# Unit 0's q and k in two parts of their tokens, and later prefetch loads, in a planned attention-and-MLP kernel

## Chip, cores and metric

The kernel runs on one core of one Trainium2 chip. The metric is the device time of one execution in microseconds (us); lower is better. Five runs of the kernel before stand beside one profiled execution of it.

## What is computed

Attention with a squared ReLU in place of the softmax, over 8 batches, 12 heads, 448 tokens and 64 columns a head; then an MLP with a squared ReLU over the 3584 tokens of all batches. Inputs and output are float32.

```python
scores = q @ k.T / sqrt(64)                      # per batch and head, 448 x 448
attn   = maximum(scores, 0) ** 2 / 448
x      = attn @ v                                # heads side by side: 3584 x 768
g      = maximum(x @ w_in, 0) ** 2               # w_in  768 x 2048
out    = g @ w_out                               # w_out 2048 x 768
```

## The kernel before

**Units and rounds.** Four heads of one batch are a unit; there are 24 units, three to a batch. Of a unit, 64 groups of seven consecutive tokens lie on partitions, so a unit has seven rounds, one for each token t of the group. q and k are loaded as float32 (raw, 448 KB each), cast to float16 (blk), and turned so that the 64 head columns lie on partitions (qkt). A round of scores (L453) multiplies one t of k by the turned q, the ReLU (L480 on VectorE or L483 on ScalarE) writes rel, the square (L487 on ScalarE or L489 on GpSimd) writes at, and the product with v (L518) collects in PSUM until it is copied to xt (L538, L540). The first MLP product of a batch reads xt (L580; L629 for the first columns of batch 0) and its squared ReLU goes to g; the second (L729 for batch 0, L794 later) makes the output, which SP's queue stores (L675).

**Three ways to load q and k.** Unit 0 is loaded by `load_qk` (L345): k on SP's queue, q on ScalarE's. Each is cast by one instruction on VectorE or ScalarE (`cast_qk`, L372), and turned on TensorE by `turn_pe` (L392, seven transposes into PSUM, in one or two calls, then a copy to qkt, L395). Units 1 to 5 are loaded by `load_early` (L362) on GpSimd's queue, which casts on the way. Units 6 to 23 are loaded by `load_qk` on SP's queue, cast on GpSimd and turned by a DMA transpose on SP's queue (`turn_dma`, L408). There are 4 raw buffers, 3 blk and 6 qkt. v and the weights come by GpSimd's queue, too (L422, L427, L432).

**The opening.** For the first 21 rounds (units 0 to 2) the query columns are worked in two parts (`PARTS`): the first 128, of the tokens QA = 0 and 1, four rounds together (the `quads`, with `tile(0, ...)`), and the other 320, of QB, a round at a time (`tile(1, ...)`). The first quad so needs tokens 0 to 3 of k and 0 and 1 of q of unit 0. The second quad needs unit 1's k and q as well.

**Zero and filler products.** Ahead of everything TensorE multiplies twelve tiles of zeros (L929, 512 columns). Until 45 us on the planner's clock, whenever it has nothing to do, a filler product of zeros (L932, 256 columns) is put in.

**The order of work.** `Plan` decides it when the program is built. Every operation has costs on the engines that can do it, dependencies, buffers, a due time, and perhaps a time `after` which it may start. TensorE's due times are `plan.now`, a running sum of costs that the `at` arguments move forward; others follow backwards from what needs them. `simulate` walks through time, gives each free engine the ready operation that is due first, and so writes the order of every queue; `land` works out when each DMA lands, from queues that share 400 KB a us and an allowance at the end, and the two are repeated five times. The times in the plan are costs of the planner, not measurements. The initial `busy` times, `{"PE": 6.25, ...}`, say from when an engine is free.

**Prefetch.** In the main loop over pairs of rounds i, `coming(n)` estimates when unit n's scores are due:

```python
def coming(n):
    return plan.now + 4.5 * (TJ * n - 2 * i) / 2
...
raws[n, w] = load_qk(n, w, max(50.0, coming(n) - 26.0), n < 8)
```

The last argument gates the loads of units 6 and 7 behind a small memset on GpSimd (L342), since their raw buffers may hold early data. On the planner's clock `coming` is 65.7 for unit 6, 75.4 for unit 7, 83.9 for unit 8 and 95.8 for unit 9, so the loads of units 6 and 7 may start at 50, those of unit 8 at 57.9 and those of unit 9 at 69.8. A load also needs a free raw buffer, which the cast of an earlier unit leaves.

Of the kernel before, what the change touches and what calls it, by code (L numbers as in the profile page):

```python
# [42 lines left out]
class Plan:  # L43
# [54 lines left out]
    def land(self):  # L98


        queues: dict = {}
        for op in sorted((op for op in self.ops if op.size), key=lambda op: op.start):
            queues.setdefault(op.engine, deque()).append([op.start + 1.3, op.size, op])
        now, idle = 0.0, set(queues)
        while queues:
            for name in idle & set(queues):
                if queues[name][0][0] <= now + 1e-9 and set(queues) - idle:
                    queues[name][0][0] = now + 2.3
                    idle.discard(name)
            live = [name for name in queues if queues[name][0][0] <= now + 1e-9]  # L110
            idle -= set(live)
            if not live:
                now = min(q[0][0] for q in queues.values())
                continue
            rate = 400e3 / len(live)
            step = min(queues[name][0][1] / rate for name in live)
            later = [q[0][0] - now for q in queues.values() if q[0][0] > now + 1e-9]
            step = min([step] + later)
            now += step
            for name in live:  # L120
                q = queues[name]
                q[0][1] -= rate * step
                if q[0][1] <= 1e-3:
                    self.landing[q.popleft()[2].id] = now + (1.2 if len(queues) > 1 else 0.9)
                    if not q or q[0][0] > now + 1e-9:
                        idle.add(name)
            queues = {name: q for name, q in queues.items() if q}
# [133 lines left out]
def kernel(  # L261
# [9 lines left out]
    nc = tc.nc  # L271

    B, H, S, D = q.shape
# [42 lines left out]
        "s": fixed(psum, "sp", 2, [P, 2, 512], FP32),  # L316
        "mm": fixed(psum, "mm", 4, [P, 512], FP32),
    }
    plan = Plan(pools, {"PE": 6.25, "ACT": 0.7, "DVE": 1.2, "POOL": 1.4, "SP": 0.7})
    plan.cold = 6.6  # L320

    def act(n, emit):
# [7 lines left out]
    def load_qk(n, w, after=0.0, gate=False):  # L330
        b, u = divmod(n, NU)
        buf = Buf("raw")

        def tile_of():
            return buf.tile

        src = (q if w == "q" else k)[b, 4 * u:4 * u + 4].rearrange(
            "(f e) (p t) d -> (e p) f (t d)", e=2, t=TJ)
        deps = []
        if gate:  # L340
            deps.append(plan.add(
                [("POOL", 0.1, 0.1, lambda: nc.gpsimd.memset(buf.tile[0:1, 0, 0:1], 0.0))],  # L342
                bufs=[buf], after=after))
        eng, name = (nc.scalar, "ACT") if (n, w) == (0, "q") else (nc.sync, "SP")
        op = plan.add([(name, 0.5, 0.5, lambda: eng.dma_start(out=tile_of(), in_=src), QK)],  # L345
                      deps, [buf], after=after)
        return op, buf, tile_of

    def load_early(n, w, after, due):

        b, u = divmod(n, NU)
        z = 2 * n - 2 + (w == "q")
        buf = early if z < NH else Buf("raw")

        def view():
            if z < NH:
                return early.tile[:, 2 * z:2 * z + 2]
            return buf.tile[:, 0].bitcast(FP16).rearrange("p (f c) -> p f c", f=2)

        src = (q if w == "q" else k)[b, 4 * u:4 * u + 4].rearrange(  # L360
            "(f e) (p t) d -> (e p) f (t d)", e=2, t=TJ)
        op = plan.add([("POOL", 0.7, 0.7, lambda: nc.gpsimd.dma_start(out=view(), in_=src), QK)],  # L362
                      [], [buf], after=after, due=due)
        return op, buf, lambda t: [
            (slice(64 * f, 64 * f + 64), view()[:, f, t * D:(t + 1) * D]) for f in range(2)]

    def cast_qk(n, w, raw, names=("POOL",)):
        load, buf, tile_of = raw
        blk = Buf("blk")

        def emit(fn):
            return lambda: fn(blk.tile.rearrange("p t (f d) -> p f t d", f=2),  # L372
                              tile_of().rearrange("p f (t d) -> p f t d", d=D))

        alts = {"POOL": ("POOL", 0.88, 0.93, emit(nc.gpsimd.tensor_copy)),
                "DVE": ("DVE", 0.56, 0.63, emit(nc.vector.tensor_copy)),
                "ACT": ("ACT", 0.85, 0.94, emit(nc.scalar.copy))}
        return plan.add([alts[x] for x in names], [load], [buf, blk]), blk, (
            lambda t: [(slice(0, P), blk.tile[:, t, :])])
# [545 lines left out]
    idle = pools["part"][0].bitcast(FP16)[:, 0:512]  # L925
    nc.vector.memset(idle, 0.0)
    make_identity(nc, ident)
    for _ in range(12):
        nc.tensor.matmul(pools["mm"][3], lhsT=idle[:, 0:P], rhs=idle, start=True, stop=True)  # L929

    plan.fill_until = 45.0
    plan.filler = lambda bank: nc.tensor.matmul(  # L932
        bank[:, 0:256], lhsT=idle[:, 0:P], rhs=idle[:, 0:256], start=True, stop=True)

    early = Buf("g")
    raws, casts = {}, {}
    for w in "kq":
        raws[0, w] = load_qk(0, w)
    plan.add([("ACT", 1.3, 1.3, lambda: None)], [raws[0, "q"][0]], due=2.0)
    for w in "kq":  # L940
        casts[0, w] = cast_qk(0, w, raws[0, w], ("DVE", "ACT"))
    for w in "kq":
        casts[1, w] = load_early(1, w, 1.4, 1.0)
    load_v(0, 1.4, 1.1)
# [4 lines left out]
    w1_ops = [load_w1(0, 1.4, 1.5)]  # L949
    w1_ops += [load_w1(i, 8.0, 1.6) for i in range(1, 4)]  # L950

    QA, QB = range(0, 2), range(2, TJ)
    rounds = [divmod(r, TJ) for r in range(STREAM)]
    first_h = deque(h_first())
    held: dict = {}
# [11 lines left out]
    def tile(part, rs, at=None):  # L967
        cols = PARTS[part]
        w = cols.stop - cols.start
        sp = Buf("s")  # L970
        op = scores(rs, [sp], cols, True, at)
        second, at = square(op, sp, len(rs) * w, "at" if part else "comb")
        for j, (n, t) in enumerate(rs):
            def view(tl, j=j, w=w, part=part):
                if not part:
                    tl = tl.rearrange("p f c -> p (f c)").rearrange("p (e c) -> p e c", e=2)
                return tl[:, :, j * w:(j + 1) * w]
            held[part, n, t] = second, at, view

    quads = [rounds[r:r + 4] for r in range(0, STREAM, 4)]  # L980
    turn_pe(0, "k", casts[0, "k"], 5.6)
    turn_pe(0, "q", casts[0, "q"], None, QA)
    for i, rs in enumerate(quads):
        tile(0, rs, 7.0 + 1.2 * i)
        if i in (0, 1):
            turn_pe(i + 1, "k", casts[i + 1, "k"])
            turn_pe(i + 1, "q", casts[i + 1, "q"], None, QA)
        if i:
            put(0, quads[i - 1])
    for n in range(NU):  # L990
        turn_pe(n, "q", casts[n, "q"], None, QB)
    tile(1, rounds[0:1])
    put(0, quads[-1])
    tile(1, rounds[1:2])
# [26 lines left out]
    def coming(n):  # L1021
        return plan.now + 4.5 * (TJ * n - 2 * i) / 2

    skipped, chain = 0, None
    for i in range(STREAM // 2, NB):
        rs = [divmod(r, TJ) for r in range(max(STREAM, 2 * i), 2 * i + 2)]
        for n in range(NU, NUN):
            if i == max(STREAM // 2, TJ * (n - 2) // 2 + 1):
                if n > 5:
                    for w in "kq":  # L1030
                        raws[n, w] = load_qk(n, w, max(50.0, coming(n) - 26.0), n < 8)
                if n > 5:
                    load_v(n, coming(n) - 6.0)
            if i == max(STREAM // 2, (TJ * (n - 1) + 1) // 2 - 2) and n > 3:
                if n >= NPE:
                    for w in "kq":
                        casts[n, w] = cast_qk(n, w, raws[n, w])
                if n < NPE:
                    for w in "kq":
                        turn_pe(n, w, casts[n, w])  # L1040
                else:
                    for w in "kq":
                        turn_dma(n, w, casts[n, w])
        todo = []
        for n, t in rs:
            sp = Buf("s")
            op = scores([(n, t)], [sp], WHOLE, False)
            todo.append((op, sp, n, t))
            if chain is not None:
                chain.glue = op  # L1050
            chain = op
        for op, sp, n, t in todo:
            second, at = square(op, sp, S)
            ats[n, t] = second, at, lambda tl: tl
        if i in avs:
            chain.glue = av(avs[i], list(range(TJ)))
            chain = chain.glue
        if i in pushes:
            push_dense(pushes[i])
        if i in avs and MERGE and i + 1 < NB:  # L1060
            skipped = 1
            continue
        nxt = min([j for j in pushes if j > i] or [NB + 2])
        run_some(max(0.0, (queued - 4.0) * (1 + skipped) / (nxt - i + skipped)))
        skipped, chain = 0, None
# [38 lines left out]
```

## Time and profile before

| what | value |
|---|---|
| median of 5 runs | 388.93 us (388.13 to 393.08) |
| the profiled execution | 388.46 us, span 386.7 us, mean granted TensorE clock 0.997 |
| TensorE busy | 376.5 us (97%) |
| ScalarE / VectorE / GpSimd busy | 277.0 / 266.3 / 173.8 us (72 / 69 / 45%) |
| chain that ended last | TensorE 89%, DMA 4%, VectorE 3%, ScalarE 2% |
| DMA | 51.34 MB, mean 133 GB/s |
| unit 0's k and q | issued at 0.75, landed after 4.3 and 4.6 us |
| first scores / first ReLU | 7.64 / 8.11 us |
| filler products (L932) | 46, from 5.98 to 36.9 us |

Times in the trace count from the start of the span. A share of busy time is an average over stages with different limits, so a stage is read by the work and the waits in it. A filler product counts as busy. SPq is SP's queue, in which a DMA's time is the time to issue it; when it lands is told apart.

### The profile page before, as it was taken

How to read it: one execution, taken by the hardware profiler on the slowest of the kernel's cores; microseconds unless marked ns; L12 is line 12 of the kernel's file. 1: busy time of each engine (PE TensorE's matmuls, PEld its weight loads, DVE VectorE, ACT ScalarE, POOL GpSimd, SP SyncE). 2: the span in 40 equal slices, each digit the busy share in tenths (PEclk: the TensorE clock that was granted, in tenths of full speed). 3: DMA queues.
4: the chain of work that ended last, by engine and by line, in shares of the span. 5: the costliest groups of instructions: out<-in, count | busy, mean ns of one | idle time of the engine just before them, and what ended most of it. 6: DMA issues, size and time to landing. Idle time of an engine off the chain costs nothing.

```text
span 386.7 us, 8379 instructions
## 1 busy us (share of the span) xinstructions
PE 376.5 (97%) x3324; PEld 200.1 (52%) x3324; DVE 266.3 (69%) x387; ACT 277.0 (72%) x413; POOL 173.8 (45%) x171
## 2 busy tenths in 40 slices
PE   8899999799999999999999999999999999999995
PEld 4556565345555445544555555544455546555563
DVE  3778789587886777676986674676886676256731
ACT  4999899598768787688876687795886785244221
POOL 8757447577745763654644643442601431001000
PEclk9999999999999999999999999999999999999998
DMA  9999998993566777667378576477472002210243
GB/s 194 198 207 190 204 262 217 193 225 94 143 128 173 158 168 132 163 163 166 51 208 165 107 172 168 90 153 179 65 115 61 3 2 53 65 26 3 56 96 94
DMA packets 69671, 51.34 MB, mean 133 GB/s; under 512 B 36864, under 2 KB 69632, under 8 KB 69632
## 3 DMA queue, kind: packets, MB, share of 16 engines
q1 hardware_dynamic: 52112, 35.86, 38.2%
q0 software_dynamic: 16928, 14.09, 25.0%
q10 hardware_dynamic: 592, 0.85, 0.7%
q8 instruction: 26, 0.43, 0.5%
q14 instruction: 13, 0.11, 0.1%
HBM read 45.61 MB, written 11.01 MB: 146 GB/s over the span
## 4 chain that ended last, share of the span: by engine, by line
PE 89%; DMA 4%; DVE 3%; ACT 2%; issue 1%; POOL 0%; POOLq 0%; DVEq 0%
PE mm L580 37%; PE mm L794 29%; PE sp L453 10%; PE mm L518 8%; DMA qkt<-blk 2%; PE mm L932 2%; DMA g<-in_q_dram 2%; DVE comb L773 1%; PE mm L629 1%; PE mm L729 1%; DVE rel L480 1%; PE mm L392 1%; ACT at L487 1%; ACT rel L483 0%; DVE part L806 0%
## 5 line engine op out<-in xcount | busy, mean ns | idle before, releaser
L580 PE MATMUL mm<-xt,w 128*128 128x448 f16 (+1 forms) x768 | 149.0, 346 | 0.0
L489 POOL TENSOR_TENSOR at<-rel 128x896 f16<-128x896 f32 (+1 forms) x49 | 79.9, 1630 | 106.2 <-ACT rel L483 84.7
L564 DVE SCALAR_TENSOR_TENSOR g<-mm,g 128x448 f16<-128x448 f32 (+1 forms) x128 | 76.7, 604 | 52.6 <-ACT g L569 52.2
L487 ACT ACTIVATE at<-rel 128x896 f16<-128x896 f32 (+1 forms) x119 | 108.2, 930 | 3.5 <-PE mm L518 2.4
L580 PEld LDWEIGHTS <-w 128*128 128x128 f16 x768 | 72.1, 98 | 70.6 <-issue 12.3
L480 DVE TENSOR_SCALAR rel<-sp 128x896 f32<-128x896 f32 (+2 forms) x86 | 89.0, 1039 | 19.8 <-PE sp L453 17.9
L569 ACT ACTIVATE g<-mm 128x448 f16<-128x448 f32 (+1 forms) x128 | 67.9, 534 | 42.8 <-PE mm L580 42.3
L483 ACT ACTIVATE rel<-sp 128x896 f32<-128x896 f32 (+2 forms) x88 | 79.2, 908 | 9.1 <-PE sp L453 8.2
L794 PEld LDWEIGHTS <-comb 128*128 128x128 f16 x416 | 39.8, 98 | 29.9 <-issue 3.7
L453 PE MATMUL sp<-qkt,qkt 64*64 64x448 f16 (+2 forms) x756 | 51.0, 338 | 3.1 <-DMA qkt<-blk 2.8
L713 ACT ACTIVATE part<-mm 128x384 f32<-128x384 f32 x40 | 19.6, 489 | 41.0 <-PE mm L794 39.3
L372 POOL CAST blk<-raw 128x896 f16<-128x896 f32 x36 | 37.7, 1058 | 23.6 <-issue 13.7
L806 DVE SCALAR_TENSOR_TENSOR part<-mm,part 128x384 f32<-128x384 f32 x52 | 28.6, 554 | 24.7 <-ACT part L713 14.7
L794 PE MATMUL mm<-wt,comb 128*128 128x384 f16 x208 | 36.8, 326 | 0.2 <-DVE comb L773 0.2
L794 PE MATMUL mm<-w,comb 128*128 128x384 f16 x208 | 36.8, 326 | 0.1
L518 PE MATMUL mm<-at,vs 64*64 64x448 f16 (+1 forms) x672 | 35.3, 343 | 0.0
L794 PEld LDWEIGHTS <-g 128*128 128x128 f16 x264 | 25.1, 98 | 19.2 <-issue 3.1
L453 PEld LDWEIGHTS <-qkt 64*64 64x64 f16 x756 | 17.7, 105 | 29.0 <-issue 24.8
L422 POOL DMA_DIRECT2D vs<-in_v_dram x48 | 29.7, 627 | 4.7 <-PE sp L453 3.7
L794 PE MATMUL mm<-w,g 128*128 128x384 f16 x176 | 30.9, 326 | 0.0
L695 POOL COPY rest<-g 128x1024 f16<-128x1024 f16 x8 | 9.8, 1228 | 44.1 <-DVE g L564 44.1
L518 PEld LDWEIGHTS <-vs 64*64 64x64 f16 x756 | 22.0, 107 | 12.9 <-issue 3.3
(61 smaller groups left out, 219.2 us busy)
## 6 DMA issues: line engine op xcount, KB each, us to landing
out_dram<-part SPq DMA_DIRECT2D x108, 96.0 KB, 2.2
raw<-in_k_dram SPq DMA_DIRECT2D x19, 448.0 KB, 3.9
raw<-in_q_dram SPq DMA_DIRECT2D x18, 448.0 KB, 4.5
vs<-in_v_dram POOLq DMA_DIRECT2D x48, 112.0 KB, 4.1
w<-in_moe_w_in_dram POOLq DMA_DIRECT2D x4, 768.0 KB, 14.5
w<-in_moe_w_out_dram POOLq DMA_DIRECT2D x4, 768.0 KB, 12.3
g<-in_k_dram POOLq DMA_DIRECT2D x4, 224.0 KB, 11.3
g<-in_q_dram POOLq DMA_DIRECT2D x4, 224.0 KB, 9.8
```

Of the source, the lines that this page charges most:

```text
L372: return lambda: fn(blk.tile.rearrange("p t (f d) -> p f t d", f=2), tile_of().rearrange("p f (t d) -> p f t d", d=D))
L422: nc.gpsimd.dma_start(out=buf.tile[64 * r:64 * r + 64], in_=src[:, u, hs])
L453: nc.tensor.matmul(sp[64 * c:64 * c + 64, e, c0:c0 + w].rearrange("p (t c) -> p t c", c=TP), lhsT=kT[r, t, 64 * e:64 * e + 64], rhs=qT[r, ...
L480: dve(n, lambda: nc.vector.tensor_scalar(out=rel(), in0=sp.tile[:, :, 0:width], scalar1=0.0, scalar2=SK, op0=ALU.max, op1=ALU.mult)),
L483: act(n, lambda: nc.scalar.activation(out=rel(), in_=sp.tile[:, :, 0:width], func=AF.Relu, scale=SK))],
L487: act(n, lambda: nc.scalar.activation(out=dst(), in_=rel(), func=AF.Square)),
L489: lambda: nc.gpsimd.tensor_mul(dst(), rel(), rel()))],
L518: nc.tensor.matmul(banks[f].tile[64 * e:64 * e + 64, c0:c0 + w], lhsT=vs[r, e ^ c, t * D:(t + 1) * D], rhs=a[r, e, :], start=(t == 0), sto ...
L564: nc.vector.scalar_tensor_tensor(out=dst, in0=src, scalar=0.0, in1=dst, op0=ALU.is_gt, op1=ALU.mult)
L569: nc.scalar.activation(out=dst, in_=src, func=AF.Square)
L580: nc.tensor.matmul(bank.tile[:, c0:c0 + w], lhsT=w1[f // 4][:, m, f % 4 * P:(f % 4 + 1) * P], rhs=xts[b].tile[:, m, cols], start=(m == 0), ...
L794: nc.tensor.matmul(buf.tile[:, 0:HALF], lhsT=lhs()[:, j, :], rhs=w[:, j, :], start=(first and j == 0), stop=(j == NH - 1), skip_group_chec ...
```

## The change

Unit 0's q and k are loaded, cast and turned in two parts each: k in tokens 0 to 3 and 4 to 6, q in tokens 0 and 1 and 2 to 6 (`load_first`). Only q's first part is issued on ScalarE's queue; k's first, k's second and q's second part follow each other on SP's. Each part is cast by itself into one blk buffer and may be cast on VectorE or ScalarE. Turning is split in the same way: k's second part is turned behind the first quad. The zero products ahead fall from 12 to 9, and the planner holds TensorE free from 5.0 instead of 6.25. The due time of the first turn falls from 5.6 to 4.9 and those of the quads from 7.0 + 1.2 i to 5.8 + 1.2 i. The planner's placeholder for ScalarE's table load (1.3 us) no longer depends on q's load. The planner's allowance for a landing becomes 1.4 where it was 1.2 (several queues) or, after 12 us, 0.9 (one queue). The loads of units 6 to 23 may start at `coming(n) - 20` instead of `coming(n) - 26`. The other edits (`n > 5` for `n >= NPE`, QA and QB moved up) change nothing, since NPE is 6.

```diff
@@ -121,7 +121,8 @@
                 q = queues[name]
                 q[0][1] -= rate * step
                 if q[0][1] <= 1e-3:
-                    self.landing[q.popleft()[2].id] = now + (1.2 if len(queues) > 1 else 0.9)
+                    self.landing[q.popleft()[2].id] = now + (
+                        1.4 if len(queues) > 1 or now > 12.0 else 0.9)
                     if not q or q[0][0] > now + 1e-9:
                         idle.add(name)
             queues = {name: q for name, q in queues.items() if q}
@@ -316,7 +317,7 @@
         "s": fixed(psum, "sp", 2, [P, 2, 512], FP32),
         "mm": fixed(psum, "mm", 4, [P, 512], FP32),
     }
-    plan = Plan(pools, {"PE": 6.25, "ACT": 0.7, "DVE": 1.2, "POOL": 1.4, "SP": 0.7})
+    plan = Plan(pools, {"PE": 5.0, "ACT": 0.7, "DVE": 1.2, "POOL": 1.4, "SP": 0.7})
     plan.cold = 6.6
 
     def act(n, emit):
@@ -363,6 +364,30 @@
                       [], [buf], after=after, due=due)
         return op, buf, lambda t: [
             (slice(64 * f, 64 * f + 64), view()[:, f, t * D:(t + 1) * D]) for f in range(2)]
+
+    def load_first(w, parts):
+
+        raw, blk = Buf("raw"), Buf("blk")
+        src = (q if w == "q" else k)[0, 0:4].rearrange(
+            "(f e) (p t) d -> (e p) f (t d)", e=2, t=TJ)
+        for z, ts in enumerate(parts):
+            cols, ts = slice(ts[0] * D, (ts[-1] + 1) * D), slice(ts[0], ts[-1] + 1)
+            size = P * 2 * (cols.stop - cols.start) * 4
+            eng, name = (nc.scalar, "ACT") if (w, z) == ("q", 0) else (nc.sync, "SP")
+            load = plan.add([(name, 0.5, 0.5, lambda eng=eng, cols=cols: eng.dma_start(
+                out=raw.tile[:, :, cols], in_=src[:, :, cols]), size)], [], [raw],
+                due=-9.0 + 2 * z + (w == "q"))
+
+            def emit(fn, cols=cols, ts=ts):
+                return lambda: fn(
+                    blk.tile[:, ts].rearrange("p t (f d) -> p f t d", f=2),
+                    raw.tile[:, :, cols].rearrange("p f (t d) -> p f t d", d=D))
+
+            n = 2 * (cols.stop - cols.start)
+            casts[0, w, z] = plan.add(
+                [("DVE", 0.07 + 0.0008 * n, 0.15 + 0.0008 * n, emit(nc.vector.tensor_copy)),
+                 ("ACT", 0.09 + 0.00085 * n, 0.19 + 0.00085 * n, emit(nc.scalar.copy))],
+                [load], [raw, blk]), blk, lambda t: [(slice(0, P), blk.tile[:, t, :])]
 
     def cast_qk(n, w, raw, names=("POOL",)):
         load, buf, tile_of = raw
@@ -925,20 +950,20 @@
     idle = pools["part"][0].bitcast(FP16)[:, 0:512]
     nc.vector.memset(idle, 0.0)
     make_identity(nc, ident)
-    for _ in range(12):
+    for _ in range(9):
         nc.tensor.matmul(pools["mm"][3], lhsT=idle[:, 0:P], rhs=idle, start=True, stop=True)
 
     plan.fill_until = 45.0
     plan.filler = lambda bank: nc.tensor.matmul(
         bank[:, 0:256], lhsT=idle[:, 0:P], rhs=idle[:, 0:256], start=True, stop=True)
 
+    QS = QA, QB = range(0, 2), range(2, TJ)
+    KA = range(0, 4), range(4, TJ)
     early = Buf("g")
     raws, casts = {}, {}
-    for w in "kq":
-        raws[0, w] = load_qk(0, w)
-    plan.add([("ACT", 1.3, 1.3, lambda: None)], [raws[0, "q"][0]], due=2.0)
-    for w in "kq":
-        casts[0, w] = cast_qk(0, w, raws[0, w], ("DVE", "ACT"))
+    for w, parts in (("k", KA), ("q", QS)):
+        load_first(w, parts)
+    plan.add([("ACT", 1.3, 1.3, lambda: None)], [], due=2.0)
     for w in "kq":
         casts[1, w] = load_early(1, w, 1.4, 1.0)
     load_v(0, 1.4, 1.1)
@@ -949,7 +974,6 @@
     w1_ops = [load_w1(0, 1.4, 1.5)]
     w1_ops += [load_w1(i, 8.0, 1.6) for i in range(1, 4)]
 
-    QA, QB = range(0, 2), range(2, TJ)
     rounds = [divmod(r, TJ) for r in range(STREAM)]
     first_h = deque(h_first())
     held: dict = {}
@@ -978,17 +1002,19 @@
             held[part, n, t] = second, at, view
 
     quads = [rounds[r:r + 4] for r in range(0, STREAM, 4)]
-    turn_pe(0, "k", casts[0, "k"], 5.6)
-    turn_pe(0, "q", casts[0, "q"], None, QA)
+    turn_pe(0, "k", casts[0, "k", 0], 4.9, KA[0])
+    turn_pe(0, "q", casts[0, "q", 0], None, QA)
     for i, rs in enumerate(quads):
-        tile(0, rs, 7.0 + 1.2 * i)
+        tile(0, rs, 5.8 + 1.2 * i)
+        if not i:
+            turn_pe(0, "k", casts[0, "k", 1], None, KA[1])
         if i in (0, 1):
             turn_pe(i + 1, "k", casts[i + 1, "k"])
             turn_pe(i + 1, "q", casts[i + 1, "q"], None, QA)
         if i:
             put(0, quads[i - 1])
     for n in range(NU):
-        turn_pe(n, "q", casts[n, "q"], None, QB)
+        turn_pe(n, "q", casts[n, "q"] if n else casts[0, "q", 1], None, QB)
     tile(1, rounds[0:1])
     put(0, quads[-1])
     tile(1, rounds[1:2])
@@ -1028,11 +1054,11 @@
             if i == max(STREAM // 2, TJ * (n - 2) // 2 + 1):
                 if n > 5:
                     for w in "kq":
-                        raws[n, w] = load_qk(n, w, max(50.0, coming(n) - 26.0), n < 8)
+                        raws[n, w] = load_qk(n, w, max(50.0, coming(n) - 20.0), n < 8)
                 if n > 5:
                     load_v(n, coming(n) - 6.0)
             if i == max(STREAM // 2, (TJ * (n - 1) + 1) // 2 - 2) and n > 3:
-                if n >= NPE:
+                if n > 5:
                     for w in "kq":
                         casts[n, w] = cast_qk(n, w, raws[n, w])
                 if n < NPE:
```

## The prediction

> **What bounds the kernel now.** I read the busy table first, then the waits of TensorE, then the stretches, then the time-ordered list around the start and around the one long wait. TensorE is the bound by share:
>
> ```profile
> PE 376.5 (97%) x3324; PEld 200.1 (52%) x3324; DVE 266.3 (69%) x387; ACT 277.0 (72%) x413; POOL 173.8 (45%) x171
> ```
>
> Its 10.2 us of idle time are few pieces. The waits of TensorE (engine, line, releaser: us in total, times, longest):
>
> ```profile
> PE sp L453 <- DMA qkt<-blk: 2.8, 1, 2.8
> PE mm L929 <- DVE part L926: 1.2, 1, 1.2
> PE mm L518 <- issue: 1.1, 1, 1.1
> ```
>
> and some 4.7 us behind the last product, which the change does not touch. Busy is not useful, though: 12 products of zeros (L929) fill 1.20 to 6.15, and 46 filler products (L932), 0.11 apart, hold 5.0 us between 5.98 and 36.9. So up to 37 us TensorE waits in disguise; after that it has real work all the time but for the 2.8 us. The stretches (span, then busy us of PE, PEld, DVE, ACT, POOL, clock, DMA share, GB/s) say who sets the pace:
>
> ```profile
> 8.11:38.37 30.26, 28.65 (x503) 16.67 (x505) 22.95 (x34) 28.64 (x43) 21.35 (x26) 1.00 1.24 198
> 38.37:60.38 22.01, 22.01 (x262) 13.25 (x259) 18.48 (x30) 20.60 (x36) 11.71 (x14) 1.00 1.21 237
> 60.38:71.74 11.36, 8.59 (x62) 4.71 (x58) 8.94 (x10) 7.62 (x11) 4.99 (x6) 1.00 1.16 177
> 71.74:381.60 309.86, 309.64 (x2449) 162.03 (x2450) 212.96 (x310) 217.27 (x323) 128.99 (x113) 1.00 0.53 116
> ```
>
> From the first square to 38.37, where the last columns of batch 0 are copied into xt and the wide L580 products can begin, ScalarE is busy 28.64 of 30.26 us. It is the bound of the opening, and it starts late. From 38 us on only TensorE's work counts, and a hole.
>
> **The start, step by step.** In order of time (start, duration):
>
> ```profile
> 5.06 0.94 ACT L372 CAST blk<-raw 128x896 f16<-128x896 f32 x1 [2.50 <-DMA raw<-in_k_dram]
> 5.34 0.82 DVE L372 CAST blk<-raw 128x896 f16<-128x896 f32 x1 [4.20 <-DMA raw<-in_q_dram]
> 6.22 0.95 PE L392 MATMUL mm<-ident,blk 128*128 128x128 f16 x14
> 6.54 1.02 DVE L395 COPY qkt<-mm 128x256 f16<-128x256 f16 x2 [0.38 <-PE mm L392]
> 7.64 0.42 PE L453 MATMUL sp<-qkt,qkt 64*64 64x128 f16 x16
> 8.11 1.76 ACT L483 ACTIVATE rel<-sp 128x1024 f32<-128x1024 f32 x2 [0.21 <-PE sp L453]
> ```
>
> The first quad needs only four tokens of k and two of q. In the change those are 256 and 128 KB of the 896 KB. *Landing:* the 896 KB took 4.6 us from issue; a 96 KB store lands in 2.2 (median), so some 2.0 are fixed and 2.6 are data; 384 KB of the data are 1.1. The parts would then land at 0.75 + 3.1 = 3.85, against 5.34; if all four parts travel interleaved nothing is gained. I take 4.3, a gain of 0.75 to 1.0 with k as the later. *Cast:* 512 of 896 elements at 0.9 ns plus 0.1 is about 0.55 against 0.82 to 0.94: 0.3. *Turn:* 6 transposes instead of the 14 ahead of the scores: 0.35 against 0.83. But zeros run at half pace: the 512 columns of an L929 product come 0.43 apart, L932's 256 columns 0.11 apart. With 9 zeros real work starts at 1.20 + 9 x 0.43 = 5.05, probably before the pace doubles (it did between 5.4 and 6.0), so the six turns cost up to 0.64; I take 0.55: 0.3 gained. *Copy:* 512 and 256 wide instead of 896 and 256: 0.2. The sum is 1.55 to 1.8; first scores at about 6.1 instead of 7.64, and cutting three zeros (1.24 us) makes room for just that. The added work, two more loads, two more casts and one more copy, is some 0.1 to 0.15 of fixed time each on ScalarE and VectorE, which both idled before 8 us; the second k and q parts stand behind k's first in SP's queue, which has nothing else to issue before 51.79.
>
> What passes through? Quad 1 needs unit 1's q, issued on GpSimd's queue at 2.33 and landed at 8.23; that does not move. Until then ScalarE and VectorE can only take unit 0's own rounds, second part, which need q's late tokens. ScalarE at 95% means that an earlier first square is worth nearly its whole shift at 38 us, if the gap until 9.8 is filled. Bounds: 0 (quad 1 decides) and -1.5. I take -1.2.
>
> In sentences that nothing else rests on: the Trainium skill, "TensorE: Matmul & The Clock Gate" (Part 1: The HAM clock gate), says the array runs at half clock until it has been busy for a window of about 3.4 us. That speaks against fewer zeros; here half pace lasted until some 4.5 us of zeros, and by the rule, with the window unluckily placed, the first scores too would run at half pace, an estimated 0.3 us more, a start gain of 0.9. The same skill's "DMA: Bandwidth & Descriptors" (Bandwidth) wants transfers of 1 MiB or more and gives each a fixed 2.0 us; if these added up for SP's three parts, q's second part would land at an estimated 8.5 us and the start gain would be about half.
>
> **The hole.** Around it, SP's queue:
>
> ```profile
> 60.30 0.37 SPq L345 DMA_DIRECT2D raw<-in_k_dram  x1
> 60.77 1.33 SPq L408 DMA_TRANSPOSE qkt<-blk  x1
> 62.19 0.52 SPq L345 DMA_DIRECT2D raw<-in_q_dram  x1
> 62.77 3.85 SPq L408 DMA_TRANSPOSE qkt<-blk  x2
> 66.67 1.86 SPq L675 DMA_DIRECT2D out_dram<-part  x3
> 68.63 2.24 SPq L408 DMA_TRANSPOSE qkt<-blk  x1
> ```
>
> k and q of unit 8 (60.30, 62.19) slip in ahead of unit 6's transposes as soon as the casts free a raw buffer. k8 lands after 3.5 us, unit 6's k transpose after 4.0 (64.8), q8 after 5.2 (67.4), and unit 6's q transpose, behind them all, after 8.8, at 71.60. TensorE had run dry at 68.96. Elsewhere a transpose lands in 3.0 (the one of 72.89). The change puts the loads of unit n at the planner's coming(n) - 20 instead of - 26; coming itself falls by 1.2 with the start's due times, so they move by +4.8: unit 8 from 57.9 to 62.7 on the planner's clock. Then the transpose of q6, issued near 62.0, has only k6's ahead and GpSimd's v loads beside it: landing after 3.0 to 4.9, at 65 to 67. TensorE, 1.2 earlier, asks at 67.8. The hole goes: -2.7; bounds 0 and -2.77. Unit 6's own loads stay at 50 us and unit 7's go from 50 to 54.2; in the trace these four landed at 58.9, 60.1, 61.2 and 62.3 in a row, the first 7.1 us after its issue at 51.79, behind w_out's last load (55.8), so a later issue of unit 7 costs nothing.
>
> What is late next: T(q7), whose cast must wait for a blk buffer, is now issued behind k8 and q8: near 66, with 5 to 7 us to land (the transposes behind loads here took 4.9 to 8.8): 71 to 75. Its scores stood at 79.53, in the new time 75.6. That holds, barely. Later units: unit 8's transposes had landed by 82.2 for scores at 94.41, 12 us to spare against 4.8; cost 0, and 0 again while that cover is there. Also queued behind a load on SP are stores, which no engine but a part buffer waits for.
>
> **The planner's two allowances** (a landing 0.2 later, 0.5 later after 12 us when alone) move orders, not work. A step set behind one or two more fillers costs 0.1 to 0.2 before 37 us; a better placed one saves as much. And every engine's order is computed anew. 0, with 0.5 either way.
>
> **Sum.** On the profiled execution's 388.46 (span 386.7): -1.2 - 2.7 = 384.56. The median of the runs stands 0.47 above that execution, so 384.9 to 385.0 on its scale; I say 384.9. A difference of about 1% is what a measurement of this kernel can tell from none; 1% below 388.93 is 385.04, so my own forecast lies on that edge.
>
> **Rivals.** *Only the hole moves* (20%): first scores are earlier, but quad 1 still waits for 8.23, ScalarE gets a gap there, and 38.37 stays. 388.93 - 2.7 = 386.2. For it: the chain of waits starts at that q load. Against: second-part rounds are ready by then. *The hole swallows the start* (12%): casts or GpSimd still put T(q6) at 71 us, an absolute time; then TensorE comes 1.2 earlier and waits 4.0. 388.9, the change doing at its second half nothing. For it: those transposes hang on loads at 50 us that don't move. Against: the two loads ahead of them do. *A new hole at unit 7* (6%): if q7's cast waits until T(k6) lands late, as in this trace (cast done 66.3), and T(q7) takes 8.8 plus q8's 5.2 in front, it lands at 80.3 against 75.6: 4.7 lost, 388.93 - 3.9 + 4.7 = 389.7, slower than before. It decides from a landing after 79.5. *More than forecast* (7%): the unexplained 1.1 us idle at 14.34, "issue", goes as well: 383.8. The forecast itself (both gains, 383.6 to 386.2) has 55%.
>
> **How the numbers follow.** Range 383.5 to 388.0: it holds the forecast, the hole alone and the larger gain, and leaves out the swallowed start and the new hole. Faster by over 1%: a little over half of the forecast's 55 and the larger gain, and a few points of the hole alone: 0.42. Slower by over 1% (beyond 392.8) needs a hole of 8 us: 0.04. The rest, 0.54, lies within 1%.
>
> **What would show it.** Right: first L453 near 6.1 to 6.4, first L483 near 6.6; the first long run of L580 products (39.23 before) at about 38; no TensorE wait on DMA qkt<-blk; k8 and q8 issued after both of unit 6's transposes; T(q6) landing in under 5 us. Wrong: first scores early, but ScalarE idle between 7 and 10; a TensorE wait over 1 us behind a transpose anywhere in 60 to 80; or more than 46 fillers.

## The result, and the profile after

The changed kernel runs in 386.79 us (median of 43 runs, 385.96 to 388.82) against 388.92 us (median of 80 runs beside it): a ratio of 0.9944 [0.9929, 0.9958], some 2.1 us or 0.6% less. The profiled execution took 387.38 us (span 385.6, mean granted clock 0.994), 1.08 less than the one before. So the time lies inside the predicted range, the difference is within 1%, and the gain is about half of the 4.0 us forecast.

Since TensorE's clock is cut to half for some microseconds in some executions of one kernel and not in others, I give beside the ratio, where less than 1% matters, the median of the executions whose mean clock is 0.9965 or more ("at full clock"): 387.4 before (65 runs, over all comparisons), 386.7 after (33 runs). This figure leaves out what an edit does to the clock itself.

TensorE's waits after (engine, line, releaser: us in total, times, longest):

```profile
PE mm L417 <- DVE blk L382: 1.5, 1, 1.5
PE mm L954 <- DVE part L951: 1.2, 1, 1.2
PE sp L478 <- ACT rel L508: 0.5, 2, 0.3
...
```

The 2.8 us behind a DMA transpose are gone, and so is the "issue" stop. New is a wait of 1.5 for a cast. SP's queue at the place of the hole:

```profile
62.06 4.18 SPq L433 DMA_TRANSPOSE qkt<-blk  x3
66.29 1.24 SPq L700 DMA_DIRECT2D out_dram<-part  x2
67.57 0.59 SPq L346 DMA_DIRECT2D raw<-in_k_dram  x1
68.21 0.48 SPq L346 DMA_DIRECT2D raw<-in_q_dram  x1
```

The loads of unit 8 now stand behind three transposes. The first two, unit 6's k and q, land 3.0 and 2.9 us after their issue; unit 6's q took 8.8 before. The third, unit 7's k (issued at 64.99), takes 7.4, with loads of v on GpSimd's queue beside it and no load of q or k under way when it was issued. The opening, in order of time (start, duration):

```profile
3.76 0.43 DVE L382 CAST blk<-raw 128x512 f16<-128x512 f32 x1 [2.62 <-DMA raw<-in_k_dram]
...
5.01 0.80 PE L417 MATMUL mm<-ident,blk 128*128 128x128 f16 x9
...
6.37 0.42 PE L478 MATMUL sp<-qkt,qkt 64*64 64x128 f16 x16
...
6.84 1.02 ACT L508 ACTIVATE rel<-sp 128x1024 f32<-128x1024 f32 x1
...
7.76 0.49 DVE L382 CAST blk<-raw 128x640 f16<-128x640 f32 x1 [3.58 <-DMA raw<-in_q_dram]
...
8.32 0.45 PE L417 MATMUL mm<-ident,blk 128*128 128x128 f16 x5 [1.53 <-DVE blk L382]
...
8.87 0.96 PE L417 MATMUL mm<-ident,g 128*64 128x128 f16 x14
...
13.17 0.42 PE L478 MATMUL sp<-qkt,qkt 64*64 64x128 f16 x16
...
40.99 3.43 PE L605 MATMUL mm<-xt,w 128*128 128x320 f16 x24
```

The first scores are 1.27 us earlier (6.37), but the second quad is at 13.17 (9.81 before) and the wide products, which end the opening, begin at 40.99 instead of 39.23: 1.76 later. Fourteen transposes that took 0.58 us before take 0.96 at 8.87. The stretch from 9 to 12 us, after and then before (span, then busy us of PE, PEld, DVE, ACT, POOL, clock, DMA share, GB/s):

```profile
9.00:12.00 3.00, 3.00 (x39) 1.75 (x38) 1.85 (x4) 0.56 (x2) 0.85 (x2) 0.50 1.26 201
```
```profile
9.00:12.00 3.00, 3.00 (x78) 2.03 (x74) 2.03 (x3) 2.94 (x5) 2.66 (x5) 1.00 1.26 201
```

TensorE is "busy" for the whole of both, but after the change it does 39 products where it did 78, at half clock, and ScalarE, the bound of the opening, works 0.56 us instead of 2.94. That is 2.4 us of the bound lost in one stretch, against 1.27 won ahead of it.

The account of the two profiled executions: opening +1.76, hole -2.77, sum -1.01; their difference is -1.08. It is an account of these two: the one before lies 1.05 above its median at full clock, the one after, with a cut clock, 0.69 above its own, and between the medians at full clock the difference is 0.7.

### The profile page after: what moved, and what is told of

Its sections match the earlier page's. It is cut to its first block, busy times and chain, and to the rows that moved or that the text cites. A ratio compares the mean times of both kernels' runs of the same rounds, so it can differ in the third digit from the quotient of the medians.

```text
span 385.6 us, 8380 instructions
## 1 busy us (share of the span) xinstructions
PE 377.2 (98%) x3322; PEld 200.4 (52%) x3322; DVE 265.0 (69%) x384; ACT 280.8 (73%) x422; POOL 168.8 (44%) x168
## 4 chain that ended last, share of the span: by engine, by line
PE 93%; DVE 3%; DMA 2%; ACT 1%; issue 0%; SPq 0%; DVEq 0%; ACTq 0%
PE mm L605 37%; PE mm L819 29%; PE sp L478 11%; PE mm L543 8%; PE mm L754 3%; DMA raw<-in_q_dram 2%; PE mm L957 2%; DVE comb L798 1%; PE mm L417 1%; PE mm L654 1%; ACT rel L508 1%; DVE rel L505 0%; DVE part L831 0%; SPq L377 0%; ACT comb L512 0%
## 5 line engine op out<-in xcount | busy, mean ns | idle before, releaser
L514 POOL TENSOR_TENSOR at<-rel 128x896 f16<-128x896 f32 (+1 forms) x45 | 72.9, 1622 | 105.5 <-ACT rel L508 70.0
L512 ACT ACTIVATE at<-rel 128x896 f16<-128x896 f32 (+1 forms) x123 | 111.6, 929 | 3.1 <-PE mm L543 2.4
L505 DVE TENSOR_SCALAR rel<-sp 128x896 f32<-128x896 f32 (+2 forms) x87 | 90.5, 1045 | 15.6 <-PE sp L478 14.5
L508 ACT ACTIVATE rel<-sp 128x896 f32<-128x896 f32 (+2 forms) x87 | 77.9, 901 | 6.2 <-PE sp L478 4.5
L397 POOL CAST blk<-raw 128x896 f16<-128x896 f32 x36 | 36.6, 1027 | 31.8 <-issue 17.6
```

The costliest lines, as they stand in the source:

```text
L505: dve(n, lambda: nc.vector.tensor_scalar(out=rel(), in0=sp.tile[:, :, 0:width], scalar1=0.0, scalar2=SK, op0=ALU.max, op1=ALU.mult)),
L508: act(n, lambda: nc.scalar.activation(out=rel(), in_=sp.tile[:, :, 0:width], func=AF.Relu, scale=SK))],
L512: act(n, lambda: nc.scalar.activation(out=dst(), in_=rel(), func=AF.Square)),
L514: lambda: nc.gpsimd.tensor_mul(dst(), rel(), rel()))],
```

## The experiments

Ratios are to the kernel before, with their 95% intervals. A run whose plan is computed anew can differ in more than its edit: orders, the engine of an operation, the number of fillers. The short names are those of the expectations.

**e1: The prefetch edit alone**, in the kernel before:

```diff
- raws[n, w] = load_qk(n, w, max(50.0, coming(n) - 26.0), n < 8)
+ raws[n, w] = load_qk(n, w, max(50.0, coming(n) - 20.0), n < 8)
```

> The kernel before with one edit: the prefetch loads may start at coming(n) - 20 instead of - 26. Theory A (the hole in front of unit 6's scores was made by the two loads that stood ahead of its transposes; the new opening loses time): the transposes of unit 6 land in about 3 us each, TensorE does not wait for them, and with the old opening (first long run of the wide product at 39.2 us) the whole 2.8 us are gained: about 386.1, ratio 0.992 to 0.994, as good as the full change or up to 0.7 better. Theory B (the gain of the change comes from its opening, the loads' place does nothing): 388.9, ratio 1.00, and the wait of 2.8 us is still there. Theory C (the hole closed only because TensorE came 1.8 us later): the wait is still over 1.5 us, 388 or more.

385.92 us, ratio 0.9957 [0.992, 0.9993]; at full clock 385.8 (9 runs), 1.6 less than before. No wait for a transpose is left: unit 8's loads are issued at 70.77 and 71.41, behind the three transposes that begin at 65.28, and unit 6's q lands at 69.80, 1.5 ahead of its first product. This one number brings at full clock more than the whole change (0.7). So loads ahead of the transposes made the hole, and the rest of the change costs about a microsecond. The profiled execution was the slowest of the twelve (390.79), with a cut clock in the opening.

```profile
65.28 4.17 SPq L408 DMA_TRANSPOSE qkt<-blk  x3
...
70.77 0.59 SPq L345 DMA_DIRECT2D raw<-in_k_dram  x1
71.41 0.47 SPq L345 DMA_DIRECT2D raw<-in_q_dram  x1
```

**e2: Everything but the prefetch edit** (the changed kernel with 26.0):

> The changed kernel with the prefetch loads put back to coming(n) - 26. Theory A: the opening is late as in the changed kernel (wide product from 41.0 us); unit 6's transposes land at an absolute time near 71 to 72, where TensorE now arrives at 70.7 instead of 69.0, so the wait shrinks to about 1 us, and the total is 388.5 to 389.5, ratio 0.999 to 1.002: no gain is left. Theory B (the gain comes from the opening): 386.8, ratio 0.994. Theory C (TensorE's later arrival closes the hole): no wait over 0.5 us, 387.0 or less.

391.43 us, ratio 1.0073 [1.0041, 1.0106]; slower than any theory had it. TensorE's waits:

```profile
PE mm L417 <- DVE blk L382: 2.5, 1, 2.5
PE sp L478 <- DMA qkt<-blk: 1.8, 1, 1.8
PE mm L819 <- DVE part L740: 1.5, 1, 1.5
...
```

The hole is back, though smaller: unit 6's q lands at 74.22, 2.6 later than before, and TensorE comes 3.6 later, since the wide products began at 42.81. The wait of 1.5 (at 113 us) for VectorE's copy out of PSUM is new. Against the changed kernel's profile that is +1.8, +1.8 and +1.5, together 5.1 of the 5.15 us between the two. At full clock 390.0 (6 runs): the start, with its planning, costs 2.6 against the kernel before, and the prefetch edit is worth 3.3 on top of it.

**e3: The allowance edit alone**, in the kernel before:

```diff
- self.landing[q.popleft()[2].id] = now + (1.2 if len(queues) > 1 else 0.9)
+ self.landing[q.popleft()[2].id] = now + (
+     1.4 if len(queues) > 1 or now > 12.0 else 0.9)
```

> The kernel before with one edit: the planner's allowance for a landing is 1.4 us instead of 1.2 or 0.9. Theory A8 (the allowance moves only orders and costs 0.5 us either way at most, as the prediction has it): 387.5 to 388.9, ratio 0.998 to 1.002, the wait in front of unit 6's scores still there. Rival A9 (the new orders put the opening back, as the planner's own count has it, the wide product 2.3 us later): wide product from 41 us or later; the wait at unit 6 then shrinks by as much, so the total is 388 to 389, or up to 390 if the wait keeps its size.

391.47 us, ratio 1.0091 [1.0054, 1.0127]; 3.9 slower at full clock. The same loads and products are in the program; the plan differs in the orders, in which engine takes some operations, and in the fillers, which are 70 instead of 46. Of TensorE's waits:

```profile
PE mm L795 <- DVE part L716: 1.5, 1, 1.5
...
PE sp L454 <- DMA qkt<-blk: 1.2, 1, 1.2
```

and, in order of time, the first wide products:

```profile
41.13 2.06 PE L581 MATMUL mm<-xt,w 128*128 128x320 f16 x14
```

The wide products start 1.9 later, the hole has moved to unit 7 (80.56 us) and shrunk from 2.8 to 1.2, and the wait of 1.5 for VectorE's copy is here too: a sum of 1.8 of the 2.8 us between the profiles. The rest I did not place.

**e12: The parts alone** (the changed kernel with the old allowance and 26.0):

> The changed kernel with the old allowance and the old prefetch: the two parts, the nine zeros and the earlier due times alone. Prediction's start step: 1.2 us faster than the kernel before, 386.2 at full clock. Theory S2: the opening is 1 to 2 us later for q's late part, and the wait in front of unit 6's scores shrinks by as much, so 387.2 to 388.4, no gain; the wait on the transpose 1 to 2 us instead of 2.8.

389.26 us, ratio 1.0025 [0.9988, 1.0061]. TensorE waits 1.8 for the transpose and 1.7 for the second part's cast; the wide products begin at 40.43, 1.2 later than before. Loading and casting in parts, by itself, shows no gain.

**e9: The changed kernel with the old allowance:**

> The changed kernel with the planner's old allowance for landings (1.2 and 0.9 us): so the two parts and the later prefetch without the third edit. The allowance alone cost the kernel before 3.9 us at full clock (387.4 to 391.3). Theory S1 (it costs here too, since it moves orders of the same opening): 383.5 to 385.5 at full clock, ratio 0.990 or less. Rival S2 (with the parts, q's late second part decides the opening, whatever the allowance): q's part lands at 7.7 again, TensorE waits 1 us or more for it, wide product from 40.5 or later, 386.3 to 387.0, as the change. Rival S3 (the allowance was right for the new opening, and without it the orders are made for data that isn't there): 387.5 or more.

386.79 us, ratio 0.9958 [0.9927, 0.999]: in the median of all runs no gain over the change. At full clock 385.5, but only 3 of 12 runs were. The wait for the part's cast was 2.05 us here, with half clock from 7.85 to 14.67.

**e11: Prefetch and allowance edits without the parts:**

> The kernel before with the new allowance and the later prefetch, without the two parts. Theory S4 (the allowance's loss is in the opening, 1.9 us, and at the transposes, the rest, which the later prefetch removes): wide product from about 41.1, no TensorE wait on a transpose: 387.3 to 388.3 at full clock. Rival S5 (the allowance's loss is spread over the whole stream and adds to everything): 389.0 to 390.0, that is 391.3 less the 1.6 that the prefetch alone gave.

387.89 us, ratio 0.998 [0.9953, 1.0007]; at full clock 387.6, 1.8 above the prefetch edit alone. There is no wait at a transpose; the wide products begin at 41.41, so this cost lies in the opening.

These six and the two kernels make a table, at full clock (runs in brackets):

| edits | without prefetch edit | with it |
|---|---|---|
| none | 387.4 (65) | 385.8 (9) |
| parts | 388.4 (2) | 385.5 (3) |
| allowance | 391.3 (10) | 387.6 (10) |
| parts and allowance | 390.0 (6) | 386.7 (33) |

The prefetch edit gains in every row, 1.6 to 3.7. The allowance costs in every pair, 1.2 to 3.9. The parts give +1.0 and -1.3 without the prefetch edit, -0.3 and -0.9 with it; the cells of 2 and 3 runs are weak. So with the new allowance on both sides, where the cells are larger, the parts gain 0.9 and 1.3; with the old one, no gain is shown.

**e4: The late part by another queue:** all of unit 0's q on ScalarE's queue.

```diff
- eng, name = (nc.scalar, "ACT") if (w, z) == ("q", 0) else (nc.sync, "SP")
+ eng, name = (nc.scalar, "ACT") if w == "q" else (nc.sync, "SP")
```

> The changed kernel with both parts of unit 0's q issued on ScalarE's queue (k's two stay on SP's), so that q's second part is second instead of third in its queue. Theory A1 (the opening loses because q's second part, landed at 7.74, holds up TensorE's queue from 6.8 to 8.3, and the clock then falls to one half from 8.7 to 12.1): the part lands by 5.5, no idle piece over 0.5 us before 10 us, the granted clock stays 1.00, the second quad's scores come at about 9.8 instead of 13.2, the wide product begins at 39.2 or earlier; 385.0 or less, ratio 0.990 or less. Theory A2 (it loses because w_in's loads are issued at 12.9 instead of 9.2): as long as a square stands ahead of some of them on GpSimd the opening is still late by 1 us or more: 386.0 to 386.8.

388.93 us, ratio 0.9983 [0.9946, 1.002]; at full clock 386.1 (4 runs), with a cut clock 389.3 (8 runs). The part lands at 5.72 and the wait for it is gone. But a stop of 1.2 us that the profile calls "issue" is back, at the place where the kernel before has it, and in the profiled execution half clock followed, 16.52 to 26.76. At full clock the mend may be worth 0.6; the median of all runs shows nothing of it.

**e5: GpSimd takes no square before 12.5 us** (on the planner's clock), so that none stands ahead of the w_in loads:

```diff
+ if eng == "POOL" and len(op.alts) > 1 and now < 12.5:
+     continue
```

> The changed kernel with one rule more in the planner: GpSimd takes no square before 12.5 us, so that the four loads of w_in are not queued behind a square that waits for VectorE. q's second part is as late as in the change. Theory A1 (the late part and the half clock are the loss): w_in's loads are issued from about 9.3, but the second quad's scores still come after 12 us, and the wide product still begins at 40.5 or later: 386.3 to 386.8, ratio 0.993 to 0.995. Theory A2 (the late w_in is the loss): the idle stretch of the DMA engines near 14 us is gone, w_in's first part lands near 18.7 instead of 20.3, and the wide product begins near 39.5: 385.3, ratio 0.991.

385.73 us, ratio 0.9939 [0.9911, 0.9967]; at full clock 385.6, 1.0 below the change. In the changed kernel GpSimd's queue has this:

```profile
11.74 1.25 POOL L514 TENSOR_TENSOR at<-rel 128x640 f16<-128x640 f32 x1 [1.86 <-DVE rel L505]
12.94 3.36 POOL L452 DMA_DIRECT2D w<-in_moe_w_in_dram  x4
```

The square waits 1.86 us for VectorE's ReLU, and four loads of weights wait behind it; in the kernel before they went out from 9.20. From 12 to 16 us the DMA engines moved 111 GB/s in the changed kernel, here 194:

```profile
12.00:16.00 4.00, 3.40 (x103) 2.28 (x100) 3.53 (x4) 3.87 (x6) 4.00 (x5) 1.00 1.24 194
```

Here the first w_in load goes out at 10.69 and the wide products begin at 40.30, 0.7 earlier than after the change. The wait for the late part (1.6) and half clock (8.55 to 11.96) are still there. That w_in's loads go out earlier is not shown to be the reason: in e7 below the first goes out at 10.97 and in e11 at 9.04, and the wide products begin at 40.88 and 41.41.

**e6: Both mends together:**

> Both mends together: the changed kernel with both parts of unit 0's q on ScalarE's queue and no square on GpSimd before 12.5 us. Theory A1 (the opening lost its gain to q's late second part): what the first mend alone gave at full clock, 386.06, less what the second alone gave against the change at full clock (386.69 to 385.64, 1.0): 385.0 to 385.6, with q's second part landed by 5.5 and the first long run of the wide product by 39.5. Rival A3 (both mends give the same thing twice, an earlier w_in; the early part of q is worth nothing): no better than the second alone, 385.6 to 386.2. In both the unexplained stop of TensorE near 14 us can come back, and with it a stretch of half clock.

386.07 us, ratio 0.9933 [0.9905, 0.9962]; at full clock 386.0, no better than either mend. They do not add: with the part early and the loads early the "issue" stop (1.4 us) is back, and the wide products begin at 40.88.

**e10: q on ScalarE's queue and the old allowance:**

> The two parts with both of q on ScalarE's queue, the old allowance and the later prefetch: the version that the runs so far point to. Theory A1 with S1: q's second part by 5.5, full clock through the opening unless TensorE's stop near 14 us comes: 384.0 to 385.3 at full clock, better than the prefetch alone (385.8). Rival: the opening is bound by unit 1's loads (q at 8.2 to 9.0) and by w_in's anyway, so nothing is gained over the prefetch alone: 385.6 to 386.2.

386.61 us, ratio 0.9948 [0.9919, 0.9977]; at full clock 386.0. The wide products begin at 40.21, and the stop is there (1.5). The same end by another way.

**e7: The plan is told when the part lands:** the loads are the same, and the plan is made for q's second part landing 2.05 later.

```diff
+ late = 2.05 if q[0][2].size == 327680 else 0.0
- self.landing[q.popleft()[2].id] = now + (
+ self.landing[q.popleft()[2].id] = late + now + (
```

> The changed kernel in which only the planner is told that q's second part lands 2.05 us later (at 7.74, as measured), so that data and queues are the same and only orders differ: unit 1's k is turned ahead of unit 0's late q, and fillers take the place of the wait. Theory A4 (the loss was the order made for an early landing: TensorE stood idle with unit 1 behind it, and its clock fell): no TensorE wait over 0.5 us before 10 us, granted clock 1.00 from 8 to 12, second quad's scores by 11.5 instead of 13.2: 385.5 to 386.2, ratio 0.992 or less. Rival A5 (the late data is the loss, whatever the order): wide product again from 40.5 or later, 386.5 to 387.2.

386.65 us, ratio 0.9955 [0.993, 0.9981]; at full clock 386.6 (11 of 12 runs). No wait for the part, and full clock from 5.42 on, yet no gain on the change: fillers and unit 1's k now come first, TensorE waits 1.1 for that k, and the second quad starts at 11.75, the wide products at 40.88. So neither the wait for the part nor the clock explains the late opening by itself: with all of both removed it is 0.1 earlier.

**e8: Twelve zero products in the changed kernel**, with TensorE free from 6.25:

> The changed kernel with 12 zero products ahead again (the planner holds TensorE until 6.25, as before); everything else as in the change. Theory A6 (the early first quad is worth nothing, because the opening is held by q's second part and by unit 1's loads): first scores near 7.6 instead of 6.4, but the idle gap ahead of the late part shrinks below 0.8 us and the clock is not halved from 8.7: 386.0 to 387.0, not slower than the change. Rival A7 (the start step of the prediction: first scores 1.25 later move everything): 387.8 to 388.1.

388.82 us, ratio 1.0003 [0.9972, 1.0034]; at full clock 387.9, 1.2 above the change. First scores at 8.53, full clock from 5.88 on in the profiled execution, and a wait of 1.3 for the part all the same: in this order the late part is turned ahead of the first scores. The wide products of this profile begin at 40.30, 0.7 earlier than after the change, though the first quad is 2.2 later; from there to the end it takes 345.7 us against 344.6. So the loss lies behind the opening, and this run does not show that the earlier first quad is worth anything.

## Why the prediction was right in one half and wrong in the other

**The hole: right.** All that was to show it came: no wait for qkt, loads of unit 8 behind unit 6's transposes, which landed in under 5 us. The size (-2.7) agrees with the account (-2.77), and the edit alone shows the cause. At full clock the edit gains only 1.6 in the kernel before; with other parts of the change in place, which stretch the hole or move it, 2.9 to 3.7. The next danger named, unit 7's q transpose behind unit 8's loads, nearly came: issued at 69.59, it took 7.7 us and landed at 77.27, past the 71 to 75 forecast. It made no stall because unit 7's first scores came at 77.53 and not at the 75.6 forecast. That is a cover of 0.26 us, and luck; the other runs with the prefetch edit have 0.8 to 3.6.

**First scores: right.** The first parts landed at 3.75 and 3.95, better than the 4.3 taken; scores came at 6.37, at full pace. That is 1.27 earlier, short of the 1.55 to 1.8 summed: the casts were done by 4.4, and the turn began at 5.01, behind the nine zero products.

**What passes through the opening: wrong, and in sign.** The step that failed is "-1.2, bounds 0 and -1.5", with 0 for the allowances beside it; between the profiles the opening measured +1.76. The two terms can't be told apart in that number. The allowance edit without any parts makes the opening as late (wide products at 41.13 in e3 and 41.41 in e11), the parts without it 1.2 later (e12), and both together 1.76: they do not add. With the new allowance on both sides the parts gain 0.9 to 1.3 at full clock, near the -1.2; with the old one they do not. So the -1.2 holds or fails with the order that the planner makes, which the sum left out. Three statements under it fell in the changed kernel's trace.

First, that the second parts "stand behind k's first in SP's queue, which has nothing else to issue". The issue was free, the landing was not. Three loads in that queue, issued from 0.75 to 1.77, landed after 3.0, 3.2 and 6.0 us; the planner had q's second part at 5.69, it came at 7.74. The chain that ended last goes through it (start, us, engine, work):

```profile
1.77 5.97 DMA raw<-in_q_dram
...
7.76 0.50 DVE blk L382
...
8.32 0.45 PE mm L417 x5
```

The landing was bounded for the first parts only, and the second ones were treated as work to fill a gap. They were work that the orders of TensorE and ScalarE had in front of unit 1's. The rule quoted ahead, from "DMA: Bandwidth & Descriptors" in the Trainium skill (Anatomy of one DMA, a fit for transfers issued from GpSimd), a fixed 2.0 us for each transfer, gave an estimated 8.5 if the fixed parts added up. The 7.74 is nearer to it than the plan's 5.69; but the first two landings, 3.0 and 3.2 us after issues half a microsecond apart, show that the fixed parts do not add, so the rule is not why. About three quarters of that part's data had moved by 5 us in the trace; the rest went by 7.35, while GpSimd's casting queue, which began at 4.14, ran beside it. Second on ScalarE's queue, the part landed at 5.72 to 5.79 (e4, e6, e10).

Second, that unit 1's q "does not move". It landed at 9.0 instead of 8.23, and was turned at 10.97 instead of soon after its landing, since in a fixed order it stands behind rounds that needed the late part.

Third, that the price of fewer zeros lies at the first scores. The skill's clock page was weighed there, with 0.3 us; the first scores ran at full pace. The clock was lost afterwards, in the gap that the late part makes. The next stretches, after and before, are the first 3.41 us of full clock:

```profile
5.27:8.69 3.42, 1.78 (x34) 1.17 (x32) 0.49 (x1) 3.06 (x5) 2.09 (x4) 1.00 1.21 193
```
```profile
5.66:9.07 3.41, 3.19 (x66) 2.11 (x65) 2.49 (x6) 1.99 (x3) 2.40 (x5) 1.00 1.25 195
```

TensorE was busy 1.78 of the 3.42 us where it had been busy 3.19, and at 8.69 the clock fell to half for 3.41 us. This is a visible loss of work, but by e7 its removal alone does not pay.

**The allowances: mis-sized.** "0, with 0.5 either way" measured +3.9 alone, +1.8 with the prefetch edit, +1.2 with that and the parts. The argument that a step moves by one or two fillers overlooked how much a plan computed anew can move: e3 has 24 fillers more, wide products 1.9 later and a new wait of 1.5 at 111 us. Of all the terms this is the one that the runs show most plainly to be mis-sized.

**The total** stayed inside the range since the hole's 2.8 is larger than the opening's 1.8. That the one covered the wrong sign of the other is luck. "Only the hole moves" (386.2) is the rival nearest to the time, but not the right story: the opening did move, to the wrong side, as two of the three signs of a wrong forecast had it (ScalarE idle after the first quad, 47 fillers instead of 46). Of the loss in the opening the runs show two edits that gain on the change at full clock, the old allowance (1.2, 3 runs; over all runs nothing) and no early square on GpSimd (1.0); each makes a new plan, so what in it gains is not isolated, and they can overlap. How the loss divides among the allowance's order, the late part, the half clock and the w_in loads stays open, since each mend brought another stop.

Two slips in the prediction carry nothing: the idle time behind the last product is 4.3 us (the product ends at 382.34 of 386.68) and not 4.7, and 384.56 plus 0.47 is 385.0 and not 384.9.

No version beat the prefetch edit alone clearly: 385.6 to 385.8 at full clock for e5 and e1; e5 has the better ratio to the kernel before, 0.9939 [0.9911, 0.9967] against 0.9957 [0.992, 0.9993], and the intervals overlap.

## What to carry to other kernels

When a transfer is split so that its first part lands sooner, work out when the last part lands, and who stands behind it in the order of every engine: here the 1.27 us won at the first scores did not reach the end of the opening. An edit to a planner's assumptions is a change of the whole order, so it is costed by a run, or with bounds as wide as the largest stall that a reordering could make, not with half a microsecond. Loads that aren't needed soon belong behind the DMA transposes that are: that one edit was the safe gain here. It moved the danger one unit on, so the cover of the next transpose is worth reading in the new trace: 0.26 us here, where it had been 6.2.

## What the runs showed of the hardware

**The clock changes on a grid of 3.41 us.** The clock record of every profile changes in steps of 3.413 us; the grid lies differently in each, with full clock first from 4.08 to 6.93 us. The halvings before the last microseconds came after steps in which TensorE was busy for 40 to 62% of the time: 1.36 to 2.13 us in nine profiles (the change 1.78; e1, below, 1.95). Windows with 2.10 (e8) and 2.18 (e7) were followed by full clock, so the edge lies near 2.1 for these small products. The window of the hole before, 67.10 to 70.50, had 1.87 and kept the clock, as did one of 1.58 in e12 (from 69.98); their products were the wide ones, so busy time alone does not decide. Two stretches of e1 (span, then busy us of PE, PEld, DVE, ACT, POOL, clock, DMA share, GB/s), ahead of the halving and in it:

```profile
13.76:17.17 3.41, 1.95 (x49) 1.06 (x44) 1.64 (x4) 3.41 (x5) 2.18 (x3) 1.00 1.23 196
20.00:24.00 4.00, 4.00 (x51) 1.69 (x44) 2.48 (x3) 1.89 (x5) 2.17 (x3) 0.50 1.24 207
```

The page "TensorE: Matmul & The Clock Gate" of the Trainium skill (Why this matters for your kernels) warns of idle gaps of about 3 us; here a stop of 1.4 us, with short ones around it, was enough. The half clock lasted 3.41, 6.83 or 10.24 us. In the profile of e1 the longest of these put the wide products at 44.19, five microseconds late.

**One program is granted different clocks.** Of 105 runs of the kernel before, 40 had a lower mean clock, with a median of 390.0 against 387.4. After the change it was 11 of 44, and these cost only 1.0 more (387.7 against 386.7). That the grid's place differs may be why, since a stop falls into one step or is shared by two; no run tested it. Part of the 2.1 us between the two medians is this: at full clock it is 0.7.

**The "issue" stop of TensorE follows a transfer of instructions.** Stops of 1.1 to 1.5 us between 14 and 17 us stand in the profiles of e1, e4, e6, e7 and e10 and of the kernel before, and shorter ones of 0.4 to 0.9 in e3, e8, e11 and e12. In all ten the stop lies right ahead of TensorE's 224th recorded product, whatever that product is, and ends 1.23 to 1.45 us after a transfer of 16 KB on the DMA queue that the profile calls "instruction" has ended. In the kernel before, that transfer runs from 13.22 to 14.20 and the stop from 14.34 to 15.43 (below, the queue from 13.2 to 13.3 us, with packets, MB and share of the DMA engines; then the products, with start and duration):

```profile
q8 instruction: 1, 0.02, 60.9%
```
```profile
13.98 0.36 PE L518 MATMUL mm<-comb,vs 64*64 64x128 f16 x11
15.43 0.27 PE L518 MATMUL mm<-comb,vs 64*64 64x128 f16 x5 [1.09 <-issue]
```

The four profiles without the stop (the change, e2, e5, e9) reach their 224th product 1.44 to 4.26 us after the transfer's end. So the stop looks like TensorE waiting for its next instructions. No run moved that boundary on purpose, so this is not shown by experiment.
